# Relu that walks PSUM straight and writes every ninth place, in one attention and gated-FFN kernel

## The chip, the cores and the metric

The kernel runs on one core of a Trainium2 chip. The core has five engines with a queue of instructions each: TensorE (PE, matrix products into PSUM), VectorE (DVE), ScalarE (ACT), GpSimd (POOL) and SyncE (SP, which here issues transfers). PSUM holds eight banks of 512 32-bit numbers in each of 128 partitions; SBUF is the working memory of the same 128 partitions. The metric is the device time of one execution in microseconds (us), median of several runs. Of the kernel before there are three runs: 179.54, 179.57 and 181.11 us, median 179.57.

## The reference, cut to what matters

```python
# batch 8, heads 8, seq 576, head_dim 64; d_model 512, d_ff 1024
kv  = einsum('bhsd,bhse->bhde', k, v)
o   = einsum('bhsd,bhde->bhse', q, kv)
x   = o / sqrt(mean(o * o, -1) + 1e-6) * g_norm     # heads side by side: (8, 576, 512)
h   = maximum(x @ w_in, 0)                          # (8, 576, 1024)
c   = conv_w[0]*h[s-1] + conv_w[1]*h[s] + conv_w[2]*h[s+1]   # along the sequence
out = (h * sigmoid(c)) @ w_out                      # (8, 576, 512)
```

The change is in the line that makes `h`.

## The kernel before

Everything after the attention lies with features in the partitions and tokens along the row. `d_ff` is cut into eight blocks `f` of 128 features, `d_model` into four blocks of 128. Two neighbouring batches share one tile `h` of 128 x 8 blocks x 2 batches x 576 tokens in bf16.

Tokens arrive in another order than they leave. A batch is loaded as 64 rows of nine tokens each (token = 9n + r, with n from 0 to 63 and r from 0 to 8), so that a transfer moves long pieces. The products up to the hidden layer have their columns sorted by r first and n second. The Relu, which copies PSUM to `h`, puts them back in sequence, because the convolution needs neighbours side by side. Of batches 6 and 7 (the set `TQ` in the code: those whose `q` is transposed by a transfer) the two halves are the even r (0, 2, 4, 6, 8: five groups of 64 columns, 320) and the odd r (1, 3, 5, 7: four groups, 256). Of batches 1 to 3 they are the first and the last 32 n of all nine r (288 columns each), and of batch 0 the first four and the last five r.

The order of work is written out by hand in the string `ORDER`: each token names an operation with its batch, block and half, and after `@` the PSUM bank or the buffer that it takes. Every engine executes its share in exactly that order, so no scheduler moves anything. The operations that matter here:

- `hs.b.f.s` (L624): four matmuls, one for each block of `d_model`, give half `s` of hidden block `f` of batch `b` in one bank.
- `rh.b.f.s` (L636): the Relu of that bank into `h`, on ACT. The bank is free when it is done.
- `ta` (L666, L667), `aa` (L672) and `ab` (L677): the three taps of the convolution on DVE; `sg` (L683): the sigmoid on ACT, in place; `mg` (L707): the product of `h` and the gate on DVE.
- `om` (L717): output matmuls of 128 tokens, one for each block `f`, 512 columns; `oh` (L742) the same in halves for the last 128 tokens. `ea`, `ed` and `eh` copy the sums to a row buffer (L723, L728, L752), and `st` and `sh` send them out from SP.

For batches 6 and 7 that gives 32 `hs` and 32 `rh`. ACT does them mixed with the sigmoids of batches 4 and 5. Behind them PE has the output matmuls of batches 4 and 5 and then those of 6 and 7, while DVE and ACT make the gates of batches 6 and 7.

Other Relus are `re` (L615, both halves of a batch at once, from a pair of banks) for batches 4 and 5 and `rp` (L650) for batch 0.

Of the kernel before, what the change touches and what calls it, by code (L numbers as in the profile page):

```python
# [134 lines left out]
def kernel(  # L135
# [16 lines left out]
    R = 9  # L152
    PS = S // R
# [444 lines left out]
    def h_of(b, f):  # L598
        if ("h", b // 2) not in T:
            T["h", b // 2] = ring("h", [P, NF, 2, S], BF16, "h")  # L600
        return T["h", b // 2][:, f, b % 2, :]
# [26 lines left out]
    @op  # L628
    def rh(b, f, s):
        ps, h = T["hs", b, f, s], h_of(b, f)  # L630
        if b in TQ:
            h, fr = h.rearrange("p (n r) -> p n r", r=R)[:, :, s::2], ps.rearrange("p (g n) -> p n g", n=PS)
        else:
            h = h[:, s * HS:(s + 1) * HS].rearrange("p (n r) -> p n r", r=R)
            fr = ps.rearrange("p (r n) -> p n r", r=R)
        nc.scalar.activation(h, fr, AX.Relu)  # L636
# [173 lines left out]
```

## Time and profile before

| what | value |
|---|---|
| median of three runs | 179.57 us (179.54 to 181.11) |
| the profiled execution | 179.97 us, of which the span of instructions is 178.2 |
| PE, matmuls | 169.2 us busy, 95% of the span |
| ACT | 150.5 us, 84% |
| DVE | 148.4 us, 83% |
| POOL | 20.5 us, 11% |
| Relus of L636, all 80 | 30.3 us busy, 0.484 us each on average |
| of these, 16 of 320 elements | 7.9 us, 0.581 each |
| 16 of 256 elements | 7.7 us, 0.559 each |
| 48 of 288 elements | 17.9 us, 0.426 each |
| mean granted clock of PE | 0.997 of full |

Busy times of one engine's neighbouring instructions overlap: the next is recorded as begun while the last is still draining. The distance between two starts is what an instruction costs a busy engine. A line such as L636 is a line of the kernel; `h<-banks` is written tile and read tile; `128x320 bf16<-128x320 f32` is the shape and type of what is written and read; a bracket at the end of a row of the timeline gives the engine's idle time before it and who ended that.

### The profile page before, as it was taken

To read this page: it belongs to the slowest core of one execution; us is meant where nothing else is said; L and a number is where in the kernel's file an instruction comes from. 1 tells how busy PE (TensorE), PEld (TensorE's weight loads), DVE (VectorE), ACT (ScalarE), POOL (GpSimd) and SP (SyncE) were. 2 spreads that over 40 slices of the span, in tenths; PEclk is the share of its full clock that TensorE was granted. 3 is DMA by queue.
4 is the path that set the end of the run, shared out by engine and by line. 5 is a ranking of instruction groups with operands and counts; after the bars stand their busy time and mean duration, and the time that the engine had idled before them with its cause. 6 is when DMAs were issued, how large, how long until landed. Compare 5 with 4: busy or idle time off the path is not lost.

```text
span 178.2 us, 5048 instructions
## 1 busy us (share of the span) xinstructions
PE 169.2 (95%) x2093; PEld 101.1 (57%) x2109; DVE 148.4 (83%) x285; ACT 150.5 (84%) x273; POOL 20.5 (11%) x32
## 2 busy tenths in 40 slices
PE   7997999799999999998999999999999999999992
PEld 2354776477557677444667864444677754444452
DVE  4686639688968879999799999988999899899740
ACT  2458798999988999999999998999699986967631
POOL 3195103100402212030000000000000000000000
PEclk9999999999999999999999999999999999999998
DMA  5999999999999999999999300404230001322885
GB/s 163 392 316 207 208 207 207 209 208 207 207 213 253 208 209 206 181 167 144 174 151 159 135 4 15 180 0 161 109 146 0 0 0 59 123 97 81 318 316 190
DMA packets 25862, 29.10 MB, mean 163 GB/s; under 512 B 5988, under 2 KB 20336, under 8 KB 25840
## 3 DMA queue, kind: packets, MB, share of 16 engines
q0 software_dynamic: 13248, 14.50, 49.0%
q1 hardware_dynamic: 12048, 13.11, 26.4%
q10 hardware_dynamic: 544, 1.18, 1.7%
q8 instruction: 16, 0.26, 0.6%
q14 instruction: 6, 0.05, 0.1%
HBM read 32.52 MB, written 9.44 MB: 235 GB/s over the span
## 4 chain that ended last, share of the span: by engine, by line
PE 78%; ACT 15%; issue 3%; DVE 2%; ACTq 0%
PE banks L717 30%; PE banks L624 15%; PE banks L609 9%; PE banks L282 5%; ACT h L636 4%; PE banks L643 4%; ACT taps L683 3%; ACT sq L505 3%; PE banks L429 2%; PE banks L456 2%; PE banks L398 2%; PE banks L524 2%; PE banks L693 2%; ACT L223 1%; ACT rs L541 1%
## 5 line engine op out<-in xcount | busy, mean ns | idle before, releaser
L717 PE MATMUL banks<-w_out_sb,h 128*128 128x512 bf16 x268 | 63.4, 380 | 0.8 <-issue 0.3
L624 PE MATMUL banks<-x,w_in_sb 128*128 128x288 bf16 (+2 forms) x320 | 43.5, 286 | 1.0 <-issue 0.6
L683 ACT ACTIVATE taps<-taps,cw 128x576 bf16<-128x576 bf16 (+1 forms) x44 | 40.9, 971 | 3.8 <-DVE taps L677 3.8
L717 PEld LDWEIGHTS <-h 128*128 128x128 bf16 x280 | 26.2, 98 | 30.3 <-issue 1.3
L624 PEld LDWEIGHTS <-w_in_sb 128*128 128x128 bf16 x320 | 30.4, 98 | 11.3 <-issue 2.0
L636 ACT ACTIVATE h<-banks 128x288 bf16<-128x288 f32 (+2 forms) x80 | 30.3, 484 | 0.4 <-PE banks L624 0.2
L707 DVE TENSOR_TENSOR h<-h,taps 128x1152 bf16<-128x1152 bf16 (+1 forms) x24 | 22.9, 954 | 6.7 <-ACT h L650 4.1
L505 ACT ACTIVATE sq<-banks 128x576 bf16<-128x576 f32 (+2 forms) x32 | 20.9, 682 | 1.3 <-PE banks L456 1.2
L677 DVE TENSOR_TENSOR taps<-taps,h 128x1152 bf16<-128x1152 bf16 (+1 forms) x22 | 21.4, 973 | 0.5
L672 DVE TENSOR_TENSOR taps<-taps 128x1152 bf16<-128x1152 bf16 (+1 forms) x22 | 21.3, 978 | 0.5
L723 ACT ACTIVATE row<-banks 128x512 f32<-128x512 f32 x25 | 14.8, 603 | 6.0 <-PE banks L717 6.0
L666 DVE TENSOR_SCALAR taps<-h,cw 128x576 bf16<-128x576 bf16 (+1 forms) x44 | 18.5, 421 | 0.3 <-ACT h L650 0.2
L667 DVE TENSOR_SCALAR taps<-h,cw 128x576 bf16<-128x576 bf16 (+1 forms) x44 | 18.5, 421 | 0.0
L552 DVE SCALAR_TENSOR_TENSOR x<-banks,cw,rs 128x576 bf16<-128x576 f32 (+2 forms) x16 | 12.9, 816 | 5.4 <-ACT rs L541 5.3
L609 PE MATMUL banks<-x,w_in_sb 128*128 128x288 bf16 x128 | 16.7, 286 | 0.1
L609 PEld LDWEIGHTS <-w_in_sb 128*128 128x128 bf16 x128 | 12.3, 98 | 4.1 <-issue 0.5
L223 ACT ACT_TABLE_LOAD x10 | 12.8, 1283 | 2.0 <-issue 1.8
L282 PE MATMUL banks<-zero 128*128 128x512 bf16 x40 | 12.7, 450 | 1.4 <-DVE zero L261 1.2
L595 DVE SCALAR_TENSOR_TENSOR x<-o,cw,banks 128x576 bf16<-128x576 f32 (+2 forms) x16 | 12.1, 808 | 0.5 <-PE banks L589 0.5
L541 ACT ACTIVATE rs<-banks,eps_sb 128x576 f32<-128x576 f32 (+2 forms) x16 | 11.6, 738 | 1.1 <-PE banks L524 1.0
L517 ACT ACTIVATE o<-banks 128x576 f32<-128x576 f32 (+2 forms) x16 | 10.5, 683 | 0.5 <-PE banks L496 0.5
L615 ACT ACTIVATE h<-banks 128x576 bf16<-128x576 f32 x16 | 10.0, 673 | 0.5 <-PE banks L609 0.5
(86 smaller groups left out, 149.2 us busy)
## 6 DMA issues: line engine op xcount, KB each, us to landing
out_dram<-row SPq DMA_DIRECT2D x35, 256.0 KB, 2.3
q_sb<-in_q_dram POOLq DMA_DIRECT2D x7, 576.0 KB, 16.4
k_sb<-in_k_dram POOLq DMA_DIRECT2D x7, 576.0 KB, 13.0
v_sb<-in_v_dram POOLq DMA_DIRECT2D x7, 576.0 KB, 15.2
stg<-in_v_dram ACTq DMA_DIRECT2D x2, 576.0 KB, 6.2
stg<-in_k_dram SPq DMA_DIRECT2D x4, 288.0 KB, 6.8
w_in_sb<-in_moe_w_in_dram POOLq DMA_DIRECT2D x2, 512.0 KB, 8.2
w_out_sb<-in_moe_w_out_dram POOLq DMA_DIRECT2D x1, 1024.0 KB, 19.5
```

The costliest lines, as they stand in the source:

```text
L282: nc.tensor.matmul(ps[:, :w], zero[:, :P], zero[:, :w], start=True, stop=True)
L505: nc.scalar.activation(T["sq", b, u, s], T["o", b, u, s], AX.Square)
L609: nc.tensor.matmul(ps[:, s, :HS], w_in_sb[:, t, f * P:(f + 1) * P], T["x", b][:, t, c0:c1], start=(t == 0), stop=(t == NT - 1))
L624: nc.tensor.matmul(ps, w_in_sb[:, t, f * P:(f + 1) * P], T["x", b][:, t, c0:c1], start=(t == 0), stop=(t == NT - 1))
L636: nc.scalar.activation(h, fr, AX.Relu)
L666: nc.vector.tensor_scalar_mul(tap[:, 0, f % 2, :n, 8:8 + S], h[:, f], cw[:, f:f + 1])
L667: nc.vector.tensor_scalar_mul(tap[:, 1, f % 2, :n, :S], h[:, f], cw[:, 2 * NF + f:2 * NF + f + 1])
L672: nc.vector.tensor_add(tap[:, 1, :, :n, :S], tap[:, 0, :, :n, 7:7 + S], tap[:, 1, :, :n, 1:1 + S])
L677: nc.vector.tensor_add(y, y, span(b, n)[:, 2 * j:2 * j + 2])
L683: nc.scalar.activation(y, y, AX.Sigmoid, scale=cw[:, NF + f:NF + f + 1])
L707: nc.vector.tensor_mul(h, h, tap_of(b, j)[:, 1, :, :n, :S])
L717: nc.tensor.matmul(T["om", p, m], h[:, f, m * P:(m + 1) * P], w_out_sb[:, f, :], start=(f == 0), stop=(f == NF - 1))
```

## The change

The Relu of batches 6 and 7 names the same places of `h` and of the bank in another order of the two inner dimensions. Before, the inner loop runs over the r of one half: five or four places of `h` that are two places apart, read from PSUM 64 columns apart. After, the inner loop runs over the 64 n of one r: PSUM is read column by column, and each place of `h` lies nine places behind the last.

```diff
     def rh(b, f, s):
         ps, h = T["hs", b, f, s], h_of(b, f)
         if b in TQ:
-            h, fr = h.rearrange("p (n r) -> p n r", r=R)[:, :, s::2], ps.rearrange("p (g n) -> p n g", n=PS)
+            h, fr = h.rearrange("p (n r) -> p r n", r=R)[:, s::2, :], ps.rearrange("p (g n) -> p g n", n=PS)
         else:
             h = h[:, s * HS:(s + 1) * HS].rearrange("p (n r) -> p n r", r=R)
             fr = ps.rearrange("p (r n) -> p n r", r=R)
         nc.scalar.activation(h, fr, AX.Relu)
```

Compared by engine, the two programs differ in 32 instructions of ACT, all of L636, whose shape goes from 64x5 and 64x4 to 5x64 and 4x64. Every other instruction, on every engine, is the same and in the same place.

## The prediction

> **What bounds the kernel now.** I read the page first: which engine is busy, and which one the chain that ended last runs through.
>
> ```profile
> span 178.2 us, 5048 instructions
> ...
> PE 169.2 (95%) x2093; PEld 101.1 (57%) x2109; DVE 148.4 (83%) x285; ACT 150.5 (84%) x273; POOL 20.5 (11%) x32
> ...
> PE 78%; ACT 15%; issue 3%; DVE 2%; ACTq 0%
> ```
>
> TensorE (PE) is the bound in general; ScalarE (ACT) holds 15% of the chain. The edit touches only the 32 Relus of batches 6 and 7, so the second view is the timeline of ACT over the stretch where they run. Its columns are start, busy time, line, first form of the group and count.
>
> ```profile
> 127.81 1.25 ACT L683 ACTIVATE taps<-taps,cw 128x1152 bf16<-128x1152 bf16 x1
> 128.96 0.49 ACT L636 ACTIVATE h<-banks 128x320 bf16<-128x320 f32 x1
> 129.31 1.24 ACT L683 ACTIVATE taps<-taps,cw 128x1152 bf16<-128x1152 bf16 x1
> 130.44 2.85 ACT L636 ACTIVATE h<-banks 128x320 bf16<-128x320 f32 x8
> 133.07 1.30 ACT L683 ACTIVATE taps<-taps,cw 128x1152 bf16<-128x1152 bf16 x1
> 134.20 1.55 ACT L636 ACTIVATE h<-banks 128x320 bf16<-128x320 f32 x4
> 135.50 1.32 ACT L683 ACTIVATE taps<-taps,cw 128x1152 bf16<-128x1152 bf16 x1
> 136.63 2.97 ACT L636 ACTIVATE h<-banks 128x320 bf16<-128x320 f32 x8
> 139.29 2.51 ACT L683 ACTIVATE taps<-taps,cw 128x1152 bf16<-128x1152 bf16 x2
> 141.56 3.05 ACT L636 ACTIVATE h<-banks 128x256 bf16<-128x256 f32 x8
> 144.34 1.54 ACT L683 ACTIVATE taps<-taps,cw 128x576 bf16<-128x576 bf16 x2
> 146.67 1.44 ACT L683 ACTIVATE taps<-taps,cw 128x576 bf16<-128x576 bf16 x2 [0.79 <-DVE taps L677]
> ```
>
> From 127.81 to 145.9 us ACT never idles (no bracket until 146.67), and 29 of the 32 Relus lie in it: 21 ahead of the sigmoid pair at 139.29, eight behind it. The other three lie later between evictions, where ACT has idle time. Third, the chain of waits in order of time, to see who needs ACT there, and PE's own timeline.
>
> ```profile
> 141.80 0.39 ACT h L636
> 142.19 0.04 issue
> 142.24 1.70 PE banks L624 x12
> ...
> 144.20 10.74 PE banks L717 x49
> 154.94 0.05 issue
> 155.00 10.74 PE banks L717 x49
> 165.74 0.05 issue
> 165.79 7.50 PE banks L717 x34
> 173.29 1.76 PE banks L742 x16
> ```
>
> ```profile
> 127.07 6.07 PE L624 MATMUL banks<-x,w_in_sb 128*128 128x320 bf16 x48
> 133.34 10.59 PE L624 MATMUL banks<-x,w_in_sb 128*128 128x320 bf16 x80 [0.20 <-ACT h L636]
> 143.77 1.03 PE L717 MATMUL banks<-w_out_sb,h 128*128 128x512 bf16 x3
> ...
> 173.13 1.91 PE L742 MATMUL banks<-w_out_sb,h 128*128 128x256 bf16 x16
> ```
>
> PE runs the matmuls that feed the Relus (L624) from 127.07 to 143.77, then output matmuls (L717) without a pause to the end. So this stage is nearly balanced: in the chain it is ACT that releases PE's banks up to 142.2. How much room PE has: fifty output matmuls of 512 columns take 10.79 us (155.00 to 165.79), 0.42 ns a column; the 128 feeding matmuls have 16x4x320 + 16x4x256 = 36,864 columns, 15.5 us at that rate against the 16.7 us taken. PE could save **1.2 us** here at most, whatever ACT does.
>
> VectorE (DVE) is the second line from ACT to the end:
>
> ```profile
> 141.83 1.36 DVE L707 TENSOR_TENSOR h<-h,taps 128x2304 bf16<-128x2304 bf16 x1 [0.48 <-ACT taps L683]
> 146.55 0.75 DVE L707 TENSOR_TENSOR h<-h,taps 128x1152 bf16<-128x1152 bf16 x1
> ...
> 168.90 0.76 DVE L707 TENSOR_TENSOR h<-h,taps 128x1152 bf16<-128x1152 bf16 x1 [0.84 <-ACT taps L683]
> ```
>
> The gating product at 141.83 waits for the sigmoid pair of 139.29; the one at 146.55 needs the pair of 144.34, done at 145.88, so it has 0.67 us to spare. The last, done at 169.66, feeds the first output matmul of feature blocks 6 and 7 of batch 7. Fourteen output matmuls (3.02 us) and sixteen half ones lie behind its two, and as the half ones begin at 173.13, its two begin at 173.13 - 14 x 0.216 = 170.1: a margin of **0.44 us**.
>
> **The change, part by part.** Nothing is moved: no DMA, queue, wait, order or count changes; 32 ACT instructions keep their 320 or 256 elements a partition. What goes is the write in 64 runs of five or four (places of h two apart, so 4 bytes) with the PSUM read jumping by 64 floats. What comes is a straight PSUM read and a write in which each place lies nine places, 18 bytes, behind the last.
>
> *The price of one Relu now.* Busy times overlap with the next instruction's start, so I take distances between starts. Full rate comes from two forms that write without gaps:
>
> ```profile
> 67.18 1.89 ACT L636 ACTIVATE h<-banks 128x288 bf16<-128x288 f32 x6
> 68.92 0.81 ACT L683 ACTIVATE taps<-taps,cw 128x576 bf16<-128x576 bf16 x1
> ...
> 78.05 1.76 ACT L505 ACTIVATE sq<-banks 128x576 bf16<-128x576 f32 x3
> 79.64 1.25 ACT L517 ACTIVATE o<-banks 128x576 f32<-128x576 f32 x2
> ```
>
> 288 elements: (68.92-67.18)/6 = 0.290 us; 576: (79.64-78.05)/3 = 0.530. So 0.833 ns an element plus 0.050. At that rate 320 elements would take 0.317 and 256 would take 0.263. Now they take 0.350 (128.96 to 129.31) and (1.30-0.35)/3 = 0.316 (the block at 134.20 is one five and three fours). So the runs cost 0.033 and 0.053 us, and removing them is worth at most that.
>
> *Which half costs it.* The 288-element form of the same line already reads PSUM in jumps (nine reads 32 floats apart, then back) and pays nothing against the straight read of L505. Reading straight on is therefore worth nothing in sight; what the fours and fives pay is most likely the gapped write. The Trainium skill, PSUM — Partial Sum Buffer, Specifications (TRN2), says that PSUM has lines of 8 bytes and that access that isn't contiguous slows matmuls considerably; if this held for ACT's reads it would put the whole 0.033 and 0.053 us on the read, and the time would be that of the first rival below. The 0.290 us row does not agree for ACT.
>
> *The price of writing every ninth place.* No row of before shows a long write of single places. The nearest rows, from both sides: gapless, 0.833 ns an element, extra nothing. Below that I see no reason to go. Short memsets put four or one place on a row:
>
> ```profile
> L268 DVE MEMSET taps<- 128x4 bf16 x2 | 0.1, 62 | 0.0
> L266 DVE MEMSET eps_sb<- 128x1 f32 x1 | 0.1, 59 | 0.0
> ```
>
> Three further places, 1168 bytes apart, cost 3 ns on DVE, 1 ns each, but so few may sit in a buffer. From the other side, the Relus of batch 0, which write four neighbours and skip five:
>
> ```profile
> 24.85 0.48 ACT L650 ACTIVATE h<-banks 128x256 bf16<-128x256 f32 x1
> ...
> 25.14 0.51 ACT L650 ACTIVATE h<-banks 128x320 bf16<-128x320 f32 x1
> ```
>
> 0.29 us for 256 elements, 0.027 over full rate, or 0.42 ns for each of 64 runs. If instead the ground covered is what sets it, (0.29-0.05)/64 = 3.75 ns goes by per 18 bytes, and in the new form each single place covers 18 bytes. So an element costs between 0.833 and 3.75 ns.
>
> I take the row nearest to it, the same instruction in the same place with fours: 0.053 us over 64 runs, **0.83 ns to open a new run**, as long as one element. In the new form each place is a run of its own, so an element costs 0.83 + 0.83 = 1.66 ns: 0.050 + 256 x 1.66 = 0.476 us for a four, 0.582 for a five, **0.160 and 0.232 us more** than now. (The fives' own opening, 0.033/64 = 0.52 ns, would give 0.08 and 0.13.) The Trainium skill, SBUF — State Buffer, Specifications (TRN2), speaks against the change: it wants at least two hits in each 16-byte line for full bandwidth, and here each line gets one; it names no price. The trace agrees in part only, since before's runs put at least three places into every 16 bytes and still pay.
>
> *The sum.* Ahead of the sigmoid pair at 139.29 lie nine fives and twelve fours: 9 x 0.232 + 12 x 0.160 = 4.0 us, and DVE's product at 141.83, which already waits for that pair, moves by all of it. The eight behind are six fives and two fours, 1.7 us, less the 0.67 to spare: 1.0. One Relu of the last three stands between sigmoid pairs: 0.2. DVE's last product is late by 5.2 us; PE had 0.44 margin: 4.8. By PE's own line: its last feeding group starts when the fourth Relu behind the pair (11 fives and 14 fours so far) frees its bank: 11 x 0.232 + 14 x 0.160 = 4.8. Both lines say **+4.8 us**, all of it waits of PE for ACT; the matmuls behind have nothing to take it up. From the profiled execution's 179.97 (span 178.2 and 1.8 around it) that is 184.8; it ran 0.4 above the median of 179.57, so 184.4 for the median.
>
> **The rivals.** *First: single places cost nothing.* Then ACT saves 11 x 0.033 + 14 x 0.053 = 1.1 us by PE's last feeding group, inside PE's room of 1.2; DVE can follow by 0.48 (its wait at 141.83) and has PE's margin of 0.44, so 0.9 in all: 178.7, the other side of before. For it: the memset rows, and that ACT's jumping reads are free. Against it: every gapped write in the trace pays something. It decides below some 1.2 ns an element.
>
> *Second: the ground covered sets it*, 3.75 ns a place: 1.01 us for a four and 1.25 for a five, 0.69 and 0.90 more. By DVE's line 9 x 0.90 + 12 x 0.69 = 16.4, plus 5.4 + 1.4 - 0.67 = 6.1, less 0.44: +22, 201.7. For it: batch 0's fives, 0.32 to 0.35 us, lie close to full rate while its fours are slower, as they would with a fixed time per 18 bytes. Against it: the fours of batches 6 and 7 cover the same ground and take 0.316, not 0.29.
>
> *Third: an opening costs what it costs in batch 0*, 0.42 ns: 0.373 and 0.452 us, 0.057 and 0.102 more. PE's line: 11 x 0.102 + 14 x 0.057 = +1.9, 181.5. For it: those writes have the 18-byte step; against it: their runs are four places long.
>
> **How the numbers follow.** Forecast (a place costs about two elements, 181.8 to 188 with openings from 0.52 ns to 1.2) 0.40; nothing extra 0.30; batch 0's opening 0.07; the ground covered, or anything from 3 ns up, 0.20; something else 0.03. One per cent, 1.8 us, is about what a measurement of this kernel can tell from no change. Faster by over that is beyond PE's room: 0.01. Within: the first rival and half the third: 0.34. Slower: the rest, 0.65. The range runs from the first rival, with 0.3 us for the runs' spread, at 178.4, up to 192 (an element at 2.5 ns, half-way in the bounds: by the working above 0.69 and 0.85 us, +12), and leaves the second rival's full size out.
>
> **What the changed profile would show.** Distances between neighbouring L636 starts near 0.48 and 0.58 us in 129 to 150 us prove the price; 0.26 and 0.32 the first rival; over 1 us the second. ACT without a pause from 127.8 on, longer idle time of PE at L624 released by ACT L636, and DVE's L707 waiting longer for ACT L683 prove the two lines; the matmuls from 144 on should be as long as now and only start later. Forms 288 of L636 and everything before 128.9 us should stay. I am wrong if the write of single places has a price of another kind than an opening, or if PE finds banks early enough that ACT's delay is not passed on.

## The result and the profile after

The changed kernel takes 205.62 us (median of six runs, 205.41 to 207.43), the kernel before 180.37 in the six runs beside them; the ratio is 1.145 (95% interval 1.138 to 1.152). Two of those six runs of before (183.80 and 185.15 us) fell into a slower state and are left out of the ratio, which compares means of 206.07 and 179.96 us. The forecast was 184.4 in a range of 178.4 to 192.0: the direction is right, the size far too small. The profiled execution took 205.66 us, 25.7 more than the one of before.

The page of the changed kernel, the lines that answer to those of before:

```profile
span 203.9 us, 5048 instructions
...
PE 175.1 (86%) x2093; PEld 102.7 (50%) x2109; DVE 148.2 (73%) x285; ACT 179.1 (88%) x273; POOL 20.5 (10%) x32
...
PE 58%; ACT 29%; DVE 4%; issue 3%; DMA 3%; POOL 0%; ACTq 0%; POOLq 0%
```

ScalarE (ACT) is 28.6 us busier and has become the busiest engine; its part in the chain goes from 15% to 29%. The timeline of ACT in the stage of the change (start, busy time, line, first form, count):

```profile
128.78 1.60 ACT L636 ACTIVATE h<-banks 128x320 bf16<-128x320 f32 x1
129.86 1.48 ACT L683 ACTIVATE taps<-taps,cw 128x1152 bf16<-128x1152 bf16 x1
131.21 10.10 ACT L636 ACTIVATE h<-banks 128x320 bf16<-128x320 f32 x8
140.76 1.51 ACT L683 ACTIVATE taps<-taps,cw 128x1152 bf16<-128x1152 bf16 x1
142.10 5.00 ACT L636 ACTIVATE h<-banks 128x320 bf16<-128x320 f32 x4
146.54 1.51 ACT L683 ACTIVATE taps<-taps,cw 128x1152 bf16<-128x1152 bf16 x1
147.89 10.39 ACT L636 ACTIVATE h<-banks 128x320 bf16<-128x320 f32 x8
157.68 2.70 ACT L683 ACTIVATE taps<-taps,cw 128x1152 bf16<-128x1152 bf16 x2
160.17 11.01 ACT L636 ACTIVATE h<-banks 128x256 bf16<-128x256 f32 x8
170.58 3.02 ACT L683 ACTIVATE taps<-taps,cw 128x576 bf16<-128x576 bf16 x4
```

The first Relu starts where it did (128.78 against 128.96), so the loss is made behind that point. The stretch from there to the sigmoids behind the 29th Relu lasts 41.8 us where it lasted 15.4. The block at 131.21, three fives and five fours, takes 9.55 us to the next start (140.76) in place of 2.63. In the middle of a block a five (a Relu of 320 elements) keeps ACT for 1.41 us from start to start and a four (256 elements) for 1.12: both are about **4.39 ns a place**, with no fixed part left. The first one after a sigmoid is cheaper, 1.08 us from 128.78 to 129.86, and the sigmoid behind it is dearer, 1.35 us to 131.21 in place of 1.14. It looks as if the writes run on behind the instruction and the next one that writes pays for what is left.

Who waits for it, from the waits between 122 us and the end (time in total, times, longest) and from the timelines of TensorE (PE) and, in the last row, VectorE (DVE):

```profile
DVE h L707 <- ACT taps L683: 25.3, 5, 10.1
...
PE banks L624 <- ACT h L636: 16.5, 12, 3.4
```

```profile
130.43 2.12 PE L624 MATMUL banks<-x,w_in_sb 128*128 128x320 bf16 x16 [0.98 <-ACT h L636]
...
165.59 0.70 PE L624 MATMUL banks<-x,w_in_sb 128*128 128x320 bf16 x4 [1.96 <-ACT h L636]
166.99 1.02 PE L717 MATMUL banks<-w_out_sb,h 128*128 128x512 bf16 x3 [0.70 <-ACT h L636]
169.82 22.61 PE L717 MATMUL banks<-w_out_sb,h 128*128 128x512 bf16 x102 [1.80 <-ACT h L636]
...
198.68 1.91 PE L742 MATMUL banks<-w_out_sb,h 128*128 128x256 bf16 x16
...
194.76 0.76 DVE L707 TENSOR_TENSOR h<-h,taps 128x1152 bf16<-128x1152 bf16 x1 [0.84 <-ACT taps L683]
```

PE waits for a bank before nearly every group of feeding matmuls. Its output matmuls start at 166.99 in place of 143.77, 23.2 us later. The fifth of them waits another 1.80 us for a bank and starts at 169.82 in place of 144.64, 25.2 us later; the half ones behind them begin 25.6 us later (198.68 and 173.13). So nearly the whole loss is made in this stage: the matmuls behind it add 0.4 us and give nothing back.

### The profile page after: what moved, and what is told of

It is laid out like the page before. It is cut to its first block, busy times and chain, and to the rows that moved or that the text cites. A ratio compares the mean times of both kernels' runs of the same rounds, so it can differ in the third digit from the quotient of the medians.

```text
span 203.9 us, 5048 instructions
## 1 busy us (share of the span) xinstructions
PE 175.1 (86%) x2093; PEld 102.7 (50%) x2109; DVE 148.2 (73%) x285; ACT 179.1 (88%) x273; POOL 20.5 (10%) x32
## 4 chain that ended last, share of the span: by engine, by line
PE 58%; ACT 29%; DVE 4%; issue 3%; DMA 3%; POOL 0%; ACTq 0%; POOLq 0%
PE banks L717 21%; ACT h L636 18%; PE banks L624 12%; PE banks L609 7%; ACT taps L683 4%; PE banks L643 4%; DMA cw_rows<-in_g_norm_dram 3%; ACT sq L505 2%; PE banks L456 2%; PE banks L398 2%; PE banks L429 2%; PE banks L524 2%; PE banks L282 2%; PE banks L693 1%; ACT L223 1%
## 5 line engine op out<-in xcount | busy, mean ns | idle before, releaser
L624 PE MATMUL banks<-x,w_in_sb 128*128 128x288 bf16 (+2 forms) x320 | 49.8, 306 | 16.9 <-ACT h L636 16.5
L636 ACT ACTIVATE h<-banks 128x288 bf16<-128x288 f32 (+2 forms) x80 | 60.2, 957 | 0.3 <-PE banks L624 0.2
L624 PEld LDWEIGHTS <-w_in_sb 128*128 128x128 bf16 x320 | 32.3, 103 | 31.7 <-issue 20.3
L707 DVE TENSOR_TENSOR h<-h,taps 128x1152 bf16<-128x1152 bf16 (+1 forms) x24 | 22.9, 954 | 30.2 <-ACT taps L683 26.0
L683 ACT ACTIVATE taps<-taps,cw 128x576 bf16<-128x576 bf16 (+1 forms) x44 | 42.0, 1001 | 2.6 <-DVE taps L677 2.5
L723 ACT ACTIVATE row<-banks 128x512 f32<-128x512 f32 x25 | 15.5, 634 | 4.2 <-PE banks L717 4.2
L609 PE MATMUL banks<-x,w_in_sb 128*128 128x288 bf16 x128 | 16.7, 286 | 0.1
L609 PEld LDWEIGHTS <-w_in_sb 128*128 128x128 bf16 x128 | 12.3, 98 | 4.1 <-issue 0.4
L282 PE MATMUL banks<-zero 128*128 128x512 bf16 x40 | 11.8, 424 | 1.4 <-DVE zero L261 1.2
```

The source lines that it names most:

```text
L282: nc.tensor.matmul(ps[:, :w], zero[:, :P], zero[:, :w], start=True, stop=True)
L609: nc.tensor.matmul(ps[:, s, :HS], w_in_sb[:, t, f * P:(f + 1) * P], T["x", b][:, t, c0:c1], start=(t == 0), stop=(t == NT - 1))
L624: nc.tensor.matmul(ps, w_in_sb[:, t, f * P:(f + 1) * P], T["x", b][:, t, c0:c1], start=(t == 0), stop=(t == NT - 1))
L683: nc.scalar.activation(y, y, AX.Sigmoid, scale=cw[:, NF + f:NF + f + 1])
L707: nc.vector.tensor_mul(h, h, tap_of(b, j)[:, 1, :, :n, :S])
```

## The experiments

**The write or the read.** The first experiment keeps the straight read and takes away the gaps of the write; h then holds the tokens of batches 6 and 7 in the order of the columns.

```diff
-            h, fr = h.rearrange("p (n r) -> p r n", r=R)[:, s::2, :], ps.rearrange("p (g n) -> p g n", n=PS)
+            h, fr = h[:, s * 320:min(s * 320 + 320, S)], ps
```

> The Relus of batches 6 and 7 read PSUM straight on, as in the changed kernel, but write gapless: h gets the tokens of these two batches in the order of the columns and not of the sequence, so what follows computes on displaced tokens. Theory (the write of single places is the whole cause): distances of 0.317 us for a five and 0.263 for a four, ScalarE saves 1.1 us against the kernel before up to TensorE's last feeding group, and the time is 0.5 to 1.0 us below the kernel before (ratio 0.994 to 0.997). Rival (reading PSUM straight on is dear in this stage, for instance because TensorE writes the next bank): distances stay at 1.1 to 1.4 us and the time near 205.

Measured: 178.97 us, ratio 0.997 to the kernel before (0.995 to 0.999). ACT's timeline:

```profile
128.46 0.43 ACT L636 ACTIVATE h<-banks 128x320 bf16<-128x320 f32 x1
128.78 1.25 ACT L683 ACTIVATE taps<-taps,cw 128x1152 bf16<-128x1152 bf16 x1
129.93 2.46 ACT L636 ACTIVATE h<-banks 128x320 bf16<-128x320 f32 x8
132.20 1.33 ACT L683 ACTIVATE taps<-taps,cw 128x1152 bf16<-128x1152 bf16 x1
```

A five takes 0.32 us (128.46 to 128.78), and the block of eight 2.27, which is what three fives at 0.317 and five fours at 0.264 make. Reading straight on costs nothing above the full rate; the write is the cause. The run also shows what gapless Relus are worth to this kernel: 0.6 us.

**The price of a gap.** The second kernel computes nothing of the model. It has groups of eight Relus of 320 elements into one buffer, with a step of k 16-bit places between two writes; L101 is k = 1, L103 k = 2, L105 k = 3, L107 k = 4, L115 k = 8, L117 k = 9, L121 k = 16, L125 is the changed kernel's five, L129 and L131 are before's five and four, L137 is a read that jumps as before's with a gapless write, and L159, L161 and L163 are steps 4, 8 and 9 on VectorE (DVE).

```python
step = lambda k, r=5: wide[:, :r * 64 * k].rearrange("p (r n k) -> p r n k", n=64, k=k)[:, :, :, 0]
...
N = range(8)
...
for _ in N:  # bf16, step 8
    nc.scalar.activation(step(8), five3, AX.Relu)
```

> Only groups of eight Relus in a row by themselves: 320 elements from one PSUM bank to bf16 places in SBUF, with the step between two places from 1 to 32 elements (2 to 64 bytes), then the very forms of after, of before and of batch 0, a jumping read with a gapless write, pairs nine places apart, 32-bit places, and the same on VectorE; nothing of the model is computed and zeros are sent out. No other engine works meanwhile. Distances between starts inside a group are what counts. Theory 'ground': the writes go out in stretches of 16 bytes, each about 4.4 ns (1.40 us / 320, as the changed kernel's fives show), so the price of a place rises with the step and stops rising at 8 elements: steps 1, 2, 4, 8, 16 give 0.32, 0.35, 0.70, 1.40, 1.40 us. Rival 'single': whatever is not right behind the last place costs 4.4 ns: 0.32, 1.40, 1.40, 1.40, 1.40. Rival 'threshold': full speed (0.32) up to 8 bytes or so and then 1.40 at once. Rival 'traffic': the price comes from the other engines' use of SBUF, and here every step gives 0.32 to 0.6 us. The read: if the jumping read with the gapless write takes 0.317 (five) and 0.263 (four), before's 0.350 and 0.316 are the write's; if it takes 0.350 and 0.316, they are the read's.

```profile
7.39 3.72 ACT L101 ACTIVATE wide<-bank 128x320 bf16<-128x320 f32 x8 [5.38 <-DVE wide L87]
11.15 4.43 ACT L103 ACTIVATE wide<-bank 128x320 bf16<-128x320 f32 x8
15.61 5.84 ACT L105 ACTIVATE wide<-bank 128x320 bf16<-128x320 f32 x8
21.48 7.25 ACT L107 ACTIVATE wide<-bank 128x320 bf16<-128x320 f32 x8
...
59.08 12.89 ACT L115 ACTIVATE wide<-bank 128x320 bf16<-128x320 f32 x8
72.01 12.74 ACT L117 ACTIVATE wide<-bank 128x320 bf16<-128x320 f32 x8
...
97.60 12.26 ACT L121 ACTIVATE wide<-bank 128x320 bf16<-128x320 f32 x8
...
145.34 4.47 ACT L129 ACTIVATE wide<-bank 128x320 bf16<-128x320 f32 x8
149.69 4.14 ACT L131 ACTIVATE wide<-bank 128x256 bf16<-128x256 f32 x8
...
161.56 3.72 ACT L137 ACTIVATE wide<-bank 128x320 bf16<-128x320 f32 x8
```

From group start to group start, divided by eight, a Relu takes 0.47 us at step 1, 0.56 at step 2, 0.73 at step 3 and 1.62 at step 8 (59.08 to 72.01 over eight); at step 16 the busy time of the eight, 12.26, gives 1.53. These Relus write one buffer and so wait for each other; 0.20 us of each is fixed (0.47 less 320 x 0.833 ns). From step 2 on the rest rises by 0.177 us with each step, 0.55 ns a place, and stops rising at step 8, where the steps put one place into 16 bytes. That is the law of the theory called ground: these 16-bit writes pay about **4.4 ns for each 16 bytes that they enter**. Step 9 and the changed kernel's own form (L125, 1.61 between starts) are on the flat part. The jumping read with the gapless write (L137) takes the 0.47 of step 1. The zeros are sent out during the first 27 us; from 59 us on, where step 8 and all that follows stand, no transfer and no other engine is busy beside a group, and the price is there all the same, which rules out their traffic as the cause. Before's forms are bound by ground too: inside their groups a five and a four both take 0.52 us (L129, L131), though without gaps the four is cheaper (0.42 against 0.47). VectorE pays the same price:

```profile
205.99 7.17 DVE L159 TENSOR_SCALAR wide<-bank 128x320 bf16<-128x320 f32 x8
213.19 12.81 DVE L161 TENSOR_SCALAR wide<-bank 128x320 bf16<-128x320 f32 x8
226.03 12.66 DVE L163 TENSOR_SCALAR wide<-bank 128x320 bf16<-128x320 f32 x8
```

Steps 4 and 8 differ by 0.705 us a piece here ((226.03-213.19)/8 less (213.19-205.99)/8), 0.55 ns a place and step as on ACT.

**What of the gap is paid for.** In the same kernel 32-bit places 16 bytes apart took only 0.76 us. The third kernel separates type, whole words and filling, with four buffers in turn so that the fixed part shrinks.

```python
def runs(i, n, k, o):    # n neighbours, k places from run to run, o places from the start
    return wides[i % 4][:, :320 // n * k].rearrange("p (a k) -> p a k", k=k)[:, :, o:o + n]
```

> Only groups of eight Relus of 320 elements by themselves, now into four buffers in turn, so that none waits for the one before it; nothing of the model is computed and zeros are sent out. What is open: 16-bit places cost 4.4 ns for each 16 bytes that are entered (1.616 us at step 8, of it 0.202 fixed), 32-bit places 16 bytes apart only (0.763-0.202)/320 = 1.75 ns. Theory 'half words': a 16-byte stretch in which a 32-bit word is written by half has to be read and put together, 4.4 ns; one written in whole words costs 1.75 ns, and one that is filled no more than its elements' 0.833 ns each. Then two neighbours on a whole word, 16 bytes apart (160 pairs) take 160 x 1.75 = 0.28, so about 0.32 us by the elements, and the same pairs one place further on (two half words) 160 x 4.4 = 0.70 us; whole-word pairs 8 bytes apart 0.32, shifted 0.35; runs of eight in every second 16 bytes 0.32, also shifted by four. 32-bit places at steps 1, 2, 3, 4, 8 take 0.32, 0.32, 0.42, 0.56, 0.56, VectorE's at step 4 also 0.56. Rival 'type': the type alone decides, and a gapped 16-bit write costs 4.4 ns for each 16 bytes, whole words or not: both pairs 16 bytes apart take 0.70. Rival 'filling': the price falls with the bytes that a stretch gets: pairs and shifted pairs alike, between 0.3 and 0.7. Reading singles nine places apart from SBUF with a gapless write: 0.32 if only writes pay, 0.5 or more if reads pay as well.

The rows are, in order: 32-bit places at steps 2, 3, 4, 6 and 8; pairs 8 bytes apart, on whole words and shifted by a place; pairs 16 bytes apart, on whole words, shifted by one and by three.

```profile
47.88 3.07 ACT L120 ACTIVATE fw<-bank 128x320 f32<-128x320 f32 x8
50.44 3.93 ACT L122 ACTIVATE fw<-bank 128x320 f32<-128x320 f32 x8
53.78 5.06 ACT L124 ACTIVATE fw<-bank 128x320 f32<-128x320 f32 x8
58.22 5.07 ACT L126 ACTIVATE fw<-bank 128x320 f32<-128x320 f32 x8
62.66 5.19 ACT L128 ACTIVATE fw<-bank 128x320 f32<-128x320 f32 x8
67.23 3.20 ACT L130 ACTIVATE wide<-bank 128x320 bf16<-128x320 f32 x8
69.81 3.67 ACT L132 ACTIVATE wide<-bank 128x320 bf16<-128x320 f32 x8
72.70 3.41 ACT L134 ACTIVATE wide<-bank 128x320 bf16<-128x320 f32 x8
75.25 6.57 ACT L136 ACTIVATE wide<-bank 128x320 bf16<-128x320 f32 x8
80.79 6.68 ACT L138 ACTIVATE wide<-bank 128x320 bf16<-128x320 f32 x8
```

One Relu takes, by the starts: 32-bit 0.32, 0.42, 0.56, 0.56, 0.57 us, so 1.75 ns for each 16 bytes entered where that is more than the elements' own time. Pairs of 16-bit places 16 bytes apart take 0.32 us (72.70 to 75.25) on whole words, the same as gapless, and 0.69 shifted by one place (75.25 to 80.79): as many bytes in as many stretches, and only the position within the 32-bit words differs. So the type doesn't decide, nor how much of the 16 bytes is filled: **16 bytes in which a 32-bit word is written by half cost 4.4 ns, those written in whole words 1.75 ns or the elements' own time.** That the half word has to be read and put together may be the reason; no run shows the inside.

Of the other forms, VectorE's 32-bit step 4 takes 0.57 us like ACT's, runs of eight in every second 16 bytes went as expected (0.32 and 0.33 shifted), and single places nine apart *read* from SBUF with a gapless write took 0.69 us where a Relu doesn't read what the one before it wrote, and 0.80 where it does. So gapped reads from SBUF pay as well; the jumping reads from PSUM that were tried don't.

**Does ACT's delay pass through in full?** The change for batch 7 alone:

```diff
-        if b in TQ:
+        if b == 7:
+            h, fr = h.rearrange("p (n r) -> p r n", r=R)[:, s::2, :], ps.rearrange("p (g n) -> p g n", n=PS)
+        elif b in TQ:
```

> The change for batch 7 alone: 16 of the 32 Relus. Theory (a fixed price of 1.06 us more for a five and 0.81 for a four, each waited for by TensorE or VectorE and nothing absorbing it): up to TensorE's last feeding group 4 fives and 6 fours, 9.1 us; by VectorE's line 2 fives and 4 fours, 5.4, then 5 fives and 2 fours less 0.67, 6.2, and one four between the sigmoids, 0.8, less 0.44, 12.0; so 12 us above the kernel before, about 191.5. Rival (the writes hinder each other only where many follow in a row, or the loss is mostly TensorE's lower clock in the long waits): well under half of the whole 25.6, under 8.

Measured 190.97 us, 11.4 above the 179.60 beside it where 12 were expected; ratio 1.063 (1.059 to 1.066). Its chain, in order of time (line numbers two higher from here on):

```profile
130.22 2.84 ACT h L638 x8
133.06 1.08 ACT taps L685
134.14 2.21 ACT h L638 x4
...
137.42 7.31 ACT h L638 x8
144.73 2.09 ACT taps L685 x2
146.82 6.12 ACT h L638 x5
```

The first block (batch 6 alone) is as long as before, the third with five Relus of batch 7 among eight takes 7.3 in place of 2.8. Half of the Relus give a little under half of the loss, as the two lines by which PE and DVE wait had it.

**A version meant to beat both.** If the Relu is to write gapless, the tokens must be sorted earlier. DVE writes x in runs of 64 columns with the nine r in sequence, and the feeding matmuls take 32 columns of each of the nine groups, so that the Relu is that of batches 1 to 3.

```diff
+        if b in TQ:
+            to = T["x", b][:, 2 * u:2 * u + 2, :].rearrange("p t (r n) -> p t r n", n=PS)[:, :, s::2, :]
+            fr, by = (a.rearrange("p t (g n) -> p t g n", n=PS) for a in (fr, by))
+            return [(to[:, t], fr[:, t], g_sb, by[:, t]) for t in range(2)]
...
+            if b in TQ:
+                x = T["x", b][:, t, :].rearrange("p (r n) -> p r n", n=PS)[:, :, s * 32:(s + 1) * 32]
             nc.tensor.matmul(
-                ps, w_in_sb[:, t, f * P:(f + 1) * P], T["x", b][:, t, c0:c1],
+                ps, w_in_sb[:, t, f * P:(f + 1) * P], x,
```

> A version meant to beat both: the tokens of batches 6 and 7 are sorted one step earlier, where VectorE writes x (runs of 64 columns, so hardly any gaps), the feeding matmuls take nine pieces of 32 columns, and the Relu reads and writes as for batches 1 to 3, gapless. VectorE's products for x are split in two, eight instructions more, since one instruction takes no third dimension. Theory: Relus 0.290 us apart, 1.3 us less of ScalarE in all; VectorE pays about 0.1 us for each split, 0.8 us, most of it ahead of the stage where it is waited for. Net between 1.0 below and 0.5 above the kernel before. Rival: the matmuls on pieces of 32 columns are slower than 0.122 us for 288 columns, or VectorE's writes in pieces are, and the version is slower by 1 us or more.

Measured 179.78 us, ratio 0.9995 (0.998 to 1.001): nothing won. DVE's eight further instructions stand on the chain ahead of the stage, and the feeding matmuls start at 127.60 in place of 127.07. The next version stretches the rows of x to 640 places, by which the even tokens' products need no split:

```diff
-            T["x", b] = ring("x", [P, NT, S], BF16, "x")
+            T["x", b] = ring("x", [P, NT, S if b not in TQ else 640], BF16, "x")
...
+            to = T["x", b][:, 2 * u:2 * u + 2, :].rearrange("p t (g e n) -> p t g e n", e=2, n=PS)[:, :, :5 - s, s, :]
+            return [(to[:, t], fr[:, t], g_sb, by[:, t]) for t in range(2)] if s else [(to, fr, g_sb, by)]
```

> The sorted version with four instructions of VectorE more in place of eight: the rows of x of batches 6 and 7 are stretched to 640 places, so that the products of the even tokens need no split. The sorted version lost on VectorE ahead of the stage (products for x 16 instead of 8) what it gained on ScalarE. Theory: half of that loss comes back, 0.2 to 0.5 us, and the time is 0.1 to 0.5 us below the kernel before (ratio 0.997 to 0.9995). Rival: VectorE isn't the reason, and the ratio stays at 0.9995 or above.

Measured 179.04 us beside 179.66, ratio 0.996 (0.995 to 0.998): a small gain, and the best of all kernels here that compute the whole. PE's timeline:

```profile
126.75 15.98 PE L637 MATMUL banks<-x,w_in_sb 128*128 128x288 bf16 x128
142.57 29.52 PE L728 MATMUL banks<-w_out_sb,h 128*128 128x512 bf16 x133
```

The 128 feeding matmuls take 15.8 us (126.75 to 142.57) in place of 16.7, and the timeline shows no wait for ACT among them. That is close to the 15.5 us of the columns alone, so the room of 1.2 us that the prediction gave PE was there, and 0.9 of it is now used.

## Why the prediction was wrong

*What bounds the kernel.* Right. ACT without a pause, PE on its banks and DVE on its sigmoids are what the changed profile shows, and with the measured price in place of the wrong one the two lines come near the result: with 1.06 us more for a five and 0.80 for a four, PE's line gives 11 x 1.06 + 14 x 0.80 = 22.9 us and DVE's 9 x 1.06 + 12 x 0.80 = 19.1, plus 6 x 1.06 + 2 x 0.80 - 0.67 = 7.3, plus 0.8 - 0.44, so 26.8, against the 25.6 measured. Each line misses something at this price. PE waits for banks in its output matmuls too (0.70 us at 166.99, 1.80 at 169.82), which its line leaves out. DVE's last product is 25.9 us late (194.76, before 168.90) and not the 27.2 that its line gives, since the first Relu behind a sigmoid is cheaper than the others and the one between the later sigmoids added next to nothing.

*The read is worth nothing.* Right, by the gapless write after a straight read and by the jumping read with a gapless write. The prediction's own two rows could not show it, because the full rate had been fitted to the same two rows. The rule of the Trainium skill, PSUM — Partial Sum Buffer, Specifications (TRN2), which speaks of matmuls, doesn't carry over to ACT's reads.

*The runs cost 0.033 and 0.053 us.* Right: without gaps fives and fours take 0.317 and 0.264.

*The price of every ninth place.* Here the prediction failed, at the step "0.83 ns to open a new run, as long as one element". An element was put at 1.66 ns and takes 4.39. The figure was made by subtracting full rate from what the fours took, as if the gaps' price came on top of the elements' time. But the two run side by side: a four of before enters 1152/16 = 72 stretches of 16 bytes, and 72 x 4.39 ns = 0.316 us is its whole duration. Its elements' 0.213 us are hidden behind the writes. What looked like 64 cheap openings was the visible rest of 72 dear writes, so there was no small price that could be spread over 256 places. For the fives 72 stretches give 0.316 as well, and by themselves, in the second kernel, fives and fours of this form do take the same time (0.52 us, of it 0.20 fixed); that a five took 0.350 in the kernel before, 0.03 more, stays open.

*The rivals.* The second, with a chance of 0.20, had the mechanism: the time goes by ground covered until each place stands alone. Its 3.75 ns for 18 bytes came from batch 0's fours, whose runs lie on whole words in every other row and so should cost less than writes of half words alone: in the second kernel they take 0.48 us from start to start against 0.52 for the fours of batches 6 and 7. That fits what was held against it, that the latter cover the same ground and take longer. With 4.39 its working gives the 26.8 above, 206.4 in place of 201.7. The range left its size out. The first rival's 0.9 us, as a gapless write shows it, is 0.6. The short memsets on DVE, taken as a sign for it, say nothing: DVE pays the same price in a long write. Three smaller slips change none of this: the second rival's sum leaves out the Relu between the later sigmoid pairs (0.7 us), the third's four comes to 0.371 us and not 0.373, and half-way between the bounds is 2.3 ns, not 2.5.

*The rule of two hits* in each 16-byte line (the Trainium skill, SBUF — State Buffer, Specifications (TRN2)) pointed the right way, and with 32-bit places it fits the numbers: two hits a line (step 2) run at full rate, and a line costs 1.75 ns, 2.1 elements' time. It does not tell the measured price for 16-bit places: where they fill half words the line costs 5.3 elements' time, and before's runs, with three to five hits in a line, paid already.

## What to carry to other kernels

Where ScalarE or VectorE writes 16-bit results to SBUF, count the 16-byte stretches that hold a half-written word, at 4.4 ns each, and compare the sum with the elements' time; the larger one counts, not the sum of both. Put a reordering on the side that reads PSUM, where jumps were free here, or write runs of whole 32-bit words: pairs on a word boundary were free even 16 bytes apart. And a small excess over full rate may be the tip of a cost that is hidden under it: before spreading it over more places, ask what its whole is.

## What the runs showed beside this

In the stages in which PE waits for banks its granted clock is lower. A table by stages of the changed kernel (the stretch, then busy time and count of PE, its weight loads, DVE, ACT and POOL, then PE's granted clock, the transfers' share and their GB/s):

```profile
122.00:128.80 6.80, 6.74 (x48) 3.89 (x47) 6.72 (x11) 5.06 (x8) 0.00 (x0) 1.00 0.29 110
128.80:144.00 15.20, 7.45 (x45) 4.83 (x44) 9.09 (x11) 15.20 (x14) 0.00 (x0) 0.78 0.13 48
144.00:170.60 26.60, 15.26 (x77) 8.75 (x77) 7.90 (x14) 26.60 (x23) 0.00 (x0) 0.81 0.00 0
```

The clock falls from 1.00 to 0.78 and 0.81 of full in the two stages of waiting, and is back at 1.00 behind them. ACT is busy without a pause in both stages (15.20 of 15.20 us and 26.60 of 26.60), so it never waited for PE there, and nothing shows that the lower clock cost time. A gapped read from SBUF, 320 single places nine apart, took at least 0.69 us (2.1 ns each); VectorE worked beside it, and no group reads that way alone.
